# Delta-rule attention with a gated convolution: chunk 1's e from a cross gram, chunk 0's y from U where it lies, chunk 0's last level product on two PSUM banks, and a new order

## The chip, the cores and the metric

One core of a Trainium2 chip runs the whole kernel. Its engines are TensorE (PE, with its weight loads shown as PEld), VectorE (DVE), ScalarE (ACT) and GpSimd (POOL); SyncE (SP), ACT and POOL issue the DMAs. The metric is device time in microseconds (us), the median of several runs; lower is better.

## The reference, cut to what matters

For each of 4 batches and 8 heads (32 independent states of 48x48), 768 steps of a delta rule run in order. Its output, laid out as 768x384 for each batch, goes through a causal convolution of 5 taps, a sigmoid gate, and two 384x384 products:

```python
for t in range(S):
    y[:, :, t] = einsum('bhd,bhde->bhe', q[:, :, t], state)
    v_old = einsum('bhde,bhd->bhe', state, kt)        # kt: k over its norm
    state = state + bt * einsum('bhd,bhe->bhde', kt, vt - v_old)
...
gate = 1 / (1 + exp(-conv(x)))                        # x: y of all heads side by side
out = (gate * (x @ w_val)) @ w_out
```

All is float32.

## The kernel before, in words

**Chunks.** The 768 steps are cut into 12 chunks of 64, and two chunks make a group (6 groups). Inside a chunk the recurrence is solved with matrices: the gram of K with itself gives a triangular 64x64 system for each of the 32 states; its inverse XX times the right side gives U, and the state is a running sum of K^T U. A "pair" is two states that lie on the upper and lower 64 partitions, so most products are 16 pairs x 2 = 32 small matmuls; a float32 matmul shows as two records in the profile.

**Stages of group g.** `kp` (K with K, L399) and `qp` (K with Q, L427) for the first two groups, `kq` (both at once, L388) for the later ones. ACT and DVE bring the K gram into GL (`kpside` L405, `kpadd` L414), DVE masks the Q gram into AQ (`att0` L433, `att` L440), and SP copies AQ into R, the right operand of y (`stack_att` L920). Then `prep(g)` (L849), nearly all on DVE: transpose in (L493), 9 to 15 steps on 128x32 for norms and coefficients (L448), rows and merges of 16x16 inverses (L516 to L550), two transposes out (L552); POOL, ACT and SP scatter the results into G64, W64 and XAB.

**Stages of chunk ch.** `tri` (L892): products `m16`, `m32`, `lev1`, `lev2`, each followed by copies out of PSUM, fill XX[ch % 3]; the copies of `lev2` are `tevac` (L615). `chain` (L925): `e` = K times the state before the chunk (none for chunk 0), `eadd` on DVE adds it to V in VT, `u` = XX times VT, six copies `uevac` bring U into Y and US, `s` adds K^T U to the state that lies in two PSUM banks SPS, two copies `sevac` bring the state into the Y of the next chunk, `y` multiplies Q and the masked Q gram (R) with state and U, `yevac` and small DMAs bring y into X. Half of U lies in US on the partitions opposite to those where Y wants it; two DMAs (`stack("U")`, L692, "LU") carry it over before `y`. `moe` (L961) is the convolution (ACT `conv`, 4 DVE `tap`s), sigmoid, `val` and `outp` products and the store; chunks 0, 1, 10 and 11 run it for 64 columns, the others for two chunks together.

**The weights** arrive as float64 bits and are turned into float32 by DVE steps (L312 to L325, "f64"), ACT and two POOL products each (L330).

**Order.** All this is recorded as about 1,555 operations with their dependences, and `ORDER` (L41), a list of numbers, is the order in which they are emitted; so it fixes the order on each engine. A -1 in it is a warm-up matmul (`keep_warm`, L1024) that computes nothing needed. `BANKS` (L110) names which of the 6 free PSUM banks PB each product takes; a bank is taken again only when its readers are done. Each engine runs its list in order, so a waiting instruction holds what stands behind it. XX has three buffers: chunk 0 fills XX[0], chunk 1 XX[1], chunk 2 XX[2].

## Time and profile before

| | us |
|---|---|
| median of 3 runs | 290.45 (289.08 to 291.03) |
| the profiled execution, its own time | 289.44 |
| its span, first to last instruction | 287.7 |
| PE busy in the span | 255.3 (89%) |
| DVE busy | 215.5 (75%) |
| ACT busy | 175.4 (61%) |
| POOL busy | 133.9 (47%) |
| mean granted clock of TensorE | 0.958 of full speed (1.0 is 2.4 GHz, 0.5 is 1.2 GHz) |

Times in the rows count from the start of the profiled core. A row of the timeline is one instruction or a merged run of equal ones: start, busy time, engine, line, operation, output and inputs by tile name with sizes, count, and in brackets how long the engine had been idle and what released it. L229 is the ACT copy helper, L231 that of DVE and POOL, L250 all small matmuls, L1025 the warm-ups; so small operations are told apart by their tiles.

### The profile page before, as it was taken

The numbers are of one execution on the slowest core, as the hardware profiler recorded it, in microseconds if no ns is written. First come the engines' busy times: TensorE is split into PE (matmuls) and PEld (weight loads), VectorE is DVE, ScalarE is ACT, GpSimd is POOL, SyncE is SP. The second block draws the span as 40 slices with busy tenths as digits, with TensorE's granted clock in tenths as the row PEclk, the third lists the DMA queues.
The fourth block names the chain that finished last, engine by engine and source line by source line (L and its number), as shares of the span: only waits on it lengthen the run. The fifth ranks groups of instructions, "written<-read, shape, count | busy, mean of one in ns | idle before, by whom it ended". The sixth has DMA issues, their size and how long they took to land.

```text
span 287.7 us, 14508 instructions
## 1 busy us (share of the span) xinstructions
PE 255.3 (89%) x6272; PEld 194.2 (67%) x6272; DVE 215.5 (75%) x492; ACT 175.4 (61%) x403; POOL 133.9 (47%) x262
## 2 busy tenths in 40 slices
PE   7976485868989989899989869999999999999993
PEld 4975484768876868756768636777666776666861
DVE  6589998997979993769976974895998805831960
ACT  1677445847886645886535756756865728874531
POOL 8858692579257357057558830654053264000000
PEclk9979559899999999999999997999999999999999
DMA  6579872745664462477643771572234246302213
GB/s 179 168 207 229 212 215 62 204 117 126 178 149 137 137 165 52 106 190 184 166 116 90 218 195 43 146 190 57 68 95 139 70 108 188 95 11 71 91 55 82
DMA packets 33536, 38.22 MB, mean 133 GB/s; under 512 B 15680, under 2 KB 24000, under 8 KB 33472
## 3 DMA queue, kind: packets, MB, share of 16 engines
q1 hardware_dynamic: 27232, 24.07, 32.5%
q0 software_dynamic: 5120, 12.59, 16.1%
q8 instruction: 49, 0.80, 1.2%
q10 hardware_dynamic: 1120, 0.64, 0.8%
q14 instruction: 15, 0.12, 0.1%
HBM read 21.35 MB, written 4.72 MB: 91 GB/s over the span
## 4 chain that ended last, share of the span: by engine, by line
PE 43%; DVE 29%; issue 8%; ACT 6%; POOL 6%; DMA 5%; SPq 1%; DVEq 0%; ACTq 0%; POOLq 0%
PE PB L250 21%; PE PB L750 11%; PE PB L741 9%; DVE GT L732 4%; DVE TLP L493 3%; DVE AQ L431 2%; DMA Y<-US 2%; ACT XX L229 2%; PE SPT L250 2%; DMA KQ<-in_kf_dram 1%; DVE PR L544 1%; DMA GL<-GL 1%; POOL KQ L247 1%; DVE TT__82 L525 1%; DVE VT L676 1%
## 5 line engine op out<-in xcount | busy, mean ns | idle before, releaser
L732 DVE SCALAR_TENSOR_TENSOR GT<-X,CW,GT 128x256 f32<-128x256 f32 (+1 forms) x96 | 59.8, 645 | 21.0 <-ACT GT L229 17.0
L741 PE MATMUL PB<-X,WV 128*128 128x256 f32 (+1 forms) x144 | 52.5, 509 | 0.0
L750 PE MATMUL PB<-WO,GT 128*128 128x384 f32 x144 | 51.5, 498 | 0.0
L229 ACT ACTIVATE XX<-PB 32x512 f32<-32x512 f32 (+1 forms) x58 | 34.1, 589 | 15.7 <-PE PB L250 12.5
L741 PEld LDWEIGHTS PB<-X,WV 128*128 128x128 f32 x144 | 26.7, 194 | 15.7 <-issue 12.6
L750 PEld LDWEIGHTS PB<-WO,GT 128*128 128x128 f32 x144 | 26.0, 189 | 15.8 <-issue 0.7
L250 PE MATMUL PB<-KQ 48*64 48x64 f32 (+1 forms) x1024 | 28.4, 252 | 2.8 <-DVE AQ L431 1.2
L250 PEld LDWEIGHTS PB<-KQ 48*64 48x64 f32 x1024 | 24.3, 138 | 5.0 <-issue 2.2
L624 POOL TENSOR_TENSOR VT<-VT,NRM 128x384 f32<-128x384 f32 x24 | 20.5, 858 | 13.3 <-DMA VT<-in_vt_dram 12.6
L237 POOL DMA_DIRECT2D KQ<-in_kf_dram x32 | 16.7, 523 | 18.9 <-PE PB L250 18.7
L250 PE MATMUL PB<-KQ,Y 128*48 128x64 f32 (+2 forms) x768 | 24.7, 220 | 0.7 <-DMA Y<-US 0.7
L229 ACT ACTIVATE Y<-SPT 48x768 f32<-48x768 f32 (+1 forms) x22 | 17.7, 803 | 12.3 <-PE SPT L250 9.3
L250 PEld LDWEIGHTS PB<-KQ,Y 128*48 128x48 f32 (+2 forms) x768 | 22.6, 123 | 2.9 <-issue 1.6
L676 DVE TENSOR_TENSOR VT<-PB,VT 128x384 f32<-128x384 f32 x22 | 11.8, 552 | 16.1 <-PE PB L250 10.2
L231 POOL COPY G<-GL 16x512 f32<-16x512 f32 x24 | 17.0, 708 | 14.5 <-ACT GL L229 7.8
L250 PE MATMUL PB<-VT,XX 64*64 64x48 f32 x768 | 14.1, 221 | 9.0 <-ACT XX L229 3.7
L229 ACT ACTIVATE OS<-PB 128x384 f32<-128x384 f32 x24 | 11.6, 490 | 16.0 <-PE PB L750 13.0
L250 PEld LDWEIGHTS PB<-VT,XX 64*64 64x64 f32 x768 | 12.6, 135 | 12.9 <-issue 6.4
L229 ACT ACTIVATE GL<-PB 128x256 f32<-128x256 f32 x40 | 14.4, 384 | 11.3 <-PE PB L250 5.9
L250 PE MATMUL PB<-XAB,G 128*64 128x32 f32 x384 | 14.3, 235 | 7.2 <-DVE XAB L231 6.5
L431 DVE TENSOR_TENSOR AQ<-PB,MASK 128x256 f32<-128x256 f32 (+1 forms) x40 | 17.7, 467 | 3.6 <-PE PB L250 3.4
L250 PEld LDWEIGHTS PB<-XAB,G 128*64 128x64 f32 x384 | 13.5, 153 | 8.0 <-POOL W L231 6.6
(123 smaller groups left out, 509.1 us busy)
## 6 DMA issues: line engine op xcount, KB each, us to landing
KQ<-AQ SPq DMA_DIRECT2D x48, 128.0 KB, 4.3
KQ<-in_qr_dram POOLq DMA_DIRECT2D x32, 96.0 KB, 3.5
KQ<-in_kf_dram POOLq DMA_DIRECT2D x32, 96.0 KB, 3.1
VT<-in_vt_dram POOLq DMA_DIRECT2D x16, 192.0 KB, 3.6
KT<-in_kt_dram POOLq DMA_DIRECT2D x16, 192.0 KB, 3.8
out_dram<-OS SPq DMA_DIRECT2D x16, 192.0 KB, 2.1
Y<-US SPq DMA_DIRECT2D x23, 96.0 KB, 2.9
...
```

What stands on the lines that cost most here:

```text
L229: A.activation(out=out, in_=in_, func=AF.Copy, **kw)
L231: eng.tensor_copy(out=out, in_=in_)
L237: G.dma_start(out=dst, in_=src)
L247: eng.memset(t, x)
L250: PE.matmul(p, lhsT, rhs, start=start, stop=stop, tile_position=(row, col), skip_group_check=True)
L431: V.tensor_tensor(out=AQ[ch % NAQ][:, HB * h + u:HB * h + u + n], in0=p, in1=MASK[h].unsqueeze(1).to_broadcast([128, n, C]), op=ALU.mult)
L493: V.transpose(out=TL, in_=t.rearrange("p u x -> p x u"))
L624: G.tensor_tensor(out=v, in0=v, in1=n.unsqueeze(2).to_broadcast([128, HB, D]), op=ALU.mult)
L676: V.tensor_tensor(out=v, in0=bank["e", ch, h][:, 0:HB * D], in1=v, op=ALU.add)
L732: V.scalar_tensor_tensor(out=g, in0=XB[p % NX][:, m, :, lo + k:lo + k + n], scalar=CW[:, m, k:k + 1], in1=g, op0=ALU.mult, op1=ALU.add)
L741: PE.matmul(d[:, 0:B * n], WV[:, k, 128 * m:128 * m + 128], XB[p % NX][:, k, :, lo + 4:lo + 4 + n], start=k == 0, stop=k == NKT - 1)
L750: PE.matmul(bank["out", p, lo, i][:, 0:DM], g[:, i] if n == 2 * C else g[:, 2 * i:2 * i + 2].rearrange("p b t -> p (b t)"), WO[:, k, :], s ...
```

## The change

It has four parts. **Cross gram:** a new product `gx` early in the program multiplies K of chunk 1 with K of chunk 0 (32 small matmuls), and two ACT copies put it into GX, which is the buffer XX[2]. Chunk 1's `e` is now GX times U of chunk 0 (`ex`, 32 small matmuls), instead of K times the state after chunk 0; so it reads U's copies and no longer the state's. Since GX holds XX[2], the blanking of XX[2] (4 POOL fills) and with it the triangle of chunk 2 come after `ex`, and their entries in the plan stand behind chain(1). **First y:** chunk 0's `y` takes each half of U where `uevac` left it (Y or US), so the two LU DMAs of chunk 0 are gone; its two products are now split by position of the pairs (`crossed`), and their copies out are 6 instead of 3. **Two banks:** chunk 0's `lev2` writes its lower half into one bank and its upper half into another; ACT's two `tevac` read one, DVE's two the other. **Order:** `ORDER` and `BANKS` are new from their first to their last row (1604 entries for 1599, 45 warm-ups for 44).

```diff
 ORDER = [
-    38, 22, 39, 42, 35, 24, 40, 41, 7, 36, 37, 21, 48, 47, 16, -1, 49, 2, -1, 45, -1, -1, 235, -1, -1, 240, -1, -1,
...
-            yield bank["lev", ch, 2][r, C * j:C * j + C], TD[r, j, :], ZS[r, j, :], 64 * a, 64 * a
+            yield bank["lev", ch, 2 if ch or not a else 3][r, C * j:C * j + C], TD[r, j, :], ZS[r, j, :], 64 * a, 64 * a
...
-        p = bank["lev", ch, 2][q:q + 32]
+        p = bank["lev", ch, 2 if ch or not a else 3][q:q + 32]
...
+    GX = XX[NXX - 1]
+
+    def l_gx(i):
+        p = bank["gx", i]
+        for j in range(HB):
+            pp = HB * (j // QB) + QB * i + j % QB
+            for a in range(2):
+                f, w = spots(pp // HB, a), above(pp, a)
+                yield p[w:w + 64, C * j:C * j + C], KF[0][f:f + D, pp, :], KF[1][f:f + D, pp, :], f, w
...
+    def gxevac(i):
+        copy(A, GX.rearrange("p (h y j) x -> p h y (j x)", h=2, y=2)[:, :, i], bank["gx", i].rearrange("p (h y) -> p h y", h=2))
+
+    def l_ex(o):
+        p = bank["e", 1, o]
+        for j, pp in enumerate(crossed(o)):
+            for a in range(2):
+                w, h = above(pp, a), pp // HB
+                t = US[0][w:w + 64, h, D * (pp % QB):D * (pp % QB) + D] if pp % HB >= QB else Y[0][w:w + 64, w // 64, pp, :]
+                yield p[64 * a:64 * a + 64, D * j:D * j + D], GX[w:w + 64, pp, :], t, w, 64 * a
...
     def y(ch, h):
         p = bank["y", ch, h]
+        if ch == 0:
+            for j, pp in enumerate(crossed(h)):
+                for a in range(2):
+                    w = above(pp, a)
+                    t = US[0][w:w + 64, pp // HB, D * (pp % QB):D * (pp % QB) + D] if pp % HB >= QB else Y[0][w:w + 64, w // 64, pp, :]
+                    mm(p[64 * a:64 * a + D, C * j:C * j + C], t, R[0][w:w + 64, w // 64, pp, :], w, 64 * a)
+            return
...
+            if g == 0:
+                toks = [("gx", o) for o in range(2)]
+                add("PE", gx, (), r=k_of(0) + k_of(1), w=toks, take=toks)
+                for o in range(2):
+                    add("ACT", gxevac, (o,), r=[toks[o]], w=["GX"], give=[toks[o]])
...
-            add("PE", e, (ch,), r=k_of(ch) + [("Y", c2, "S", x, v) for x in range(2) for v in range(2)], w=toks, take=toks)
+            if ch == 1:
+                add("PE", ex, (), r=["GX"] + [("Y", 0, "U", 0, v, h) for v in range(2) for h in range(2)] + [("U", 0, h) for h in range(2)],
+                    w=toks, take=toks, kind="e")
+            else:
+                add("PE", e, (ch,), r=k_of(ch) + [("Y", c2, "S", x, v) for x in range(2) for v in range(2)], w=toks, take=toks)
...
-        for v in range(2):
+        for v in range(2 if ch else 0):
             add("ACT" if last and v else "SP", stack, ("U", ch, v), r=[("U", c2, h) for h in range(2)], w=[("Y", c2, "U", 1, v)], kind="LU")
...
+            for o, e_ in ((1, 1), (1, 0), (0, 0)) if ch == 0 else ():
+                add("ACT", yevac0, (h, o, e_), r=[t], w=[("YSB", 0)] if e_ else [("X", 0, 0, k) for k in ((1,) if o else (0, 2))], give=[t], kind="yevac")
...
-    for i in range(2, NXX):
-        blank_xx(i)
...
-        if ch + 2 < NCH:
+        if 1 < ch < NCH - 2:
             tri(ch + 2)
...
         chain(ch)
+        if ch == 1:
+            blank_xx(NXX - 1)
+            tri(2)
+            tri(3)
```

**Place 1: DVE at the start of prep(1).** GL_71 is the gram of group 1, AQ_67 and AQ_66 the masked Q grams of chunks 3 and 2, OS and X_91 raw weights. Before:

```order
L417 SCALAR_TENSOR_TENSOR GL_71<-PB_117,QUAD,GL_71 128x256
L431 TENSOR_TENSOR AQ_67<-PB_120,MASK_110 128x512
L431 TENSOR_TENSOR AQ_66<-PB_121,MASK_109 128x512
L493 STREAM_TRANSPOSE TLP<-GL_71 128x1024
L459 TENSOR_SCALAR SQ<-TLP 128x32
L453 RECIPROCAL REC<-SQ 128x32
```

After:

```order
L432 TENSOR_TENSOR AQ_67<-PB_117,MASK_109 128x512
L418 SCALAR_TENSOR_TENSOR GL_71<-PB_119,QUAD,GL_71 128x256
L326 TENSOR_SCALAR GT<-OS 128x384
L418 SCALAR_TENSOR_TENSOR GL_71<-PB_118,QUAD,GL_71 128x256
L418 SCALAR_TENSOR_TENSOR GL_71<-PB_120,QUAD,GL_71 128x256
L494 STREAM_TRANSPOSE TLP<-GL_71 128x1024
L432 TENSOR_TENSOR AQ_66<-PB_121,MASK_110 128x512
L460 TENSOR_SCALAR SQ<-TLP 128x32
```

Three of the four gram additions of group 1 stood inside prep(0) before and stand right ahead of prep(1)'s transpose now; a masking of chunk 2's Q gram (AQ_66) has moved between the transpose and the coefficient steps. On PE its product (`qp` of chunk 2) stood ahead of chunk 0's triangle and now stands inside it, between `m32` and `lev1`.

**Place 2: ACT at the end of chunk 0's triangle.** XX_74 and XX_75 are the buffers of chunks 0 and 1. Before:

```order
L229 ACTIVATE ZS<-PB_117 128x8x32
L229 ACTIVATE XX_75<-PB_120 128x2x8x32
L229 ACTIVATE TD<-PB_120,QUAD 128x8x32
L229 ACTIVATE XX_74<-PB_121 32x512 x2
L229 ACTIVATE TD<-PB_120,QUAD 128x8x32
```

After:

```order
L230 ACTIVATE XX_75<-PB_118 128x2x8x32
L230 ACTIVATE TD<-PB_118,QUAD 128x8x32
L230 ACTIVATE XX_74<-PB_121 32x512
L230 ACTIVATE TD<-PB_118,QUAD 128x8x32
L230 ACTIVATE XX_74<-PB_121 32x512
```

The order on ACT is nearly the same; DVE's two copies into XX_74 read PB_121 too before, and PB_117 now.

**Place 3: DVE around chunk 1's eadd** (VT_65 is chunk 1's V). Before:

```order
L532 TENSOR_TENSOR PR_83<-TLP,TT__82 128x256
L676 TENSOR_TENSOR VT_65<-PB_118,VT_65 128x384
L676 TENSOR_TENSOR VT_65<-PB_117,VT_65 128x384
L325 TENSOR_SCALAR GT<-OS 128x384
L537 TENSOR_REDUCE ZT<-PR_83 128x2x32
```

After:

```order
L523 TENSOR_TENSOR PR_83<-TT__82,TLP 128x144
L526 TENSOR_REDUCE TT__82<-PR_83 128x4x6
L321 TENSOR_SCALAR OS<-OS 128x384
L712 TENSOR_TENSOR VT_65<-PB_117,VT_65 128x2x192
L712 TENSOR_TENSOR VT_65<-PB_119,VT_65 128x384
L523 TENSOR_TENSOR PR_83<-TT__82,TLP 128x196
```

The two additions stood behind the last row of prep(1) and most of its first merge; they stand ahead of the last row now.

## Rows read from the trace of the kernel before

**Rows 1.** Windows: stretch and length; busy us (instructions) by engine; clock, DMA.

```profile
32.00:38.00 6.00, 5.30 (x95) 5.33 (x96) 5.80 (x14) 3.24 (x8) 4.47 (x8) 0.50 0.63 143
...
69.00:110.00 41.00, 38.22 (x957) 30.70 (x958) 36.10 (x93) 29.34 (x71) 21.86 (x39) 1.00 0.56 144
110.00:250.00 140.00, 133.70 (x3474) 96.06 (x3472) 102.33 (x228) 88.94 (x206) 64.02 (x112) 0.99 0.49 126
```

**Rows 2.** Waits of PE from 26 to 69 us: total, times, longest.

```profile
PE PB L250 <- DVE XAB L231: 6.5, 1, 6.5
PE PB L250 <- ACT XX L229: 3.3, 2, 2.6
```

**Rows 3.** Timeline, DVE: two of three gram additions inside prep(0), a weight step.

```profile
20.31 0.48 DVE L417 SCALAR_TENSOR_TENSOR GL<-PB,QUAD,GL 128x256 f32<-128x256 f32 x1
...
21.11 0.48 DVE L417 SCALAR_TENSOR_TENSOR GL<-PB,QUAD,GL 128x256 f32<-128x256 f32 x1 [0.32 <-ACT GL L229]
...
31.62 0.40 DVE L318 TENSOR_SCALAR OS<-OS 128x384 f32<-128x384 f32 x1
```

**Rows 4.** Timeline, PE: two qp products, then lev1, lev2 of chunk 0 and a warm-up.

```profile
24.00 2.22 PE L250 MATMUL PB<-KQ 48*64 48x64 f32 x128 [0.20 <-DMA KQ<-in_qr_dram]
...
39.00 1.07 PE L250 MATMUL PB<-XX,GL 32*32 32x32 f32 x64 [0.69 <-ACT XX L229]
...
42.23 1.27 PE L250 MATMUL PB<-ZS,TD 64*64 64x64 f32 x32
...
44.19 0.49 PE L1025 MATMUL SPT<-ZW 128*128 128x128 f32 x2
```

**Rows 5.** Timeline: the copies of lev2(0) on DVE and ACT, then u(0) on PE.

```profile
45.16 1.40 DVE L231 COPY XX<-PB 32x512 f32<-32x512 f32 x2
...
46.59 1.20 ACT L229 ACTIVATE XX<-PB 32x512 f32<-32x512 f32 x2 [2.52 <-DVE XX L231]
...
47.32 1.20 PE L250 MATMUL PB<-VT,XX 64*64 64x48 f32 x64 [2.65 <-ACT XX L229]
```

**Rows 6.** Timeline: chunk 1 from the last copies of U to its own u.

```profile
49.96 1.01 ACT L229 ACTIVATE Y<-PB 64x192 f32<-64x192 f32 x3
...
53.05 1.10 PE L250 MATMUL PB<-KQ 48*64 48x128 f32 x32
...
53.16 1.63 ACT L229 ACTIVATE Y<-SPT 48x768 f32<-48x768 f32 x2 [1.00 <-PE SPT L1025]
...
54.84 1.33 PE L250 MATMUL PB<-Y,KQ 48*64 48x48 f32 x60 [0.52 <-ACT Y L229]
...
58.15 1.02 DVE L676 TENSOR_TENSOR VT<-PB,VT 128x384 f32<-128x384 f32 x2
...
58.85 1.15 PE L250 MATMUL PB<-VT,XX 64*64 64x48 f32 x64 [1.73 <-DVE VT L676]
```

**Rows 7.** Timeline: ACT's DMA issues ahead of chunk 2's e, e(2), chunk 2's m16.

```profile
63.45 1.63 ACTq L240 DMA_DIRECT2D X<-YSB  x2
...
67.21 1.50 PE L250 MATMUL PB<-Y,KQ 48*64 48x48 f32 x64
...
69.17 1.12 PE L250 MATMUL PB<-XAB,G 128*64 128x32 f32 x32 [0.45 <-ACT GL L229]
```

**Rows 8.** Timeline: the longest PE wait behind 69 us, and val before and after.

```profile
165.69 2.84 PE L741 MATMUL PB<-X,WV 128*128 128x512 f32 x6
...
171.05 1.14 PE L250 MATMUL PB<-VT,XX 64*64 64x48 f32 x62 [2.28 <-DVE GT L745]
172.12 4.54 PE L741 MATMUL PB<-X,WV 128*128 128x512 f32 x6
```

**Rows 9.** Timeline, DVE and POOL: one coefficient form alone and beside POOL.

```profile
14.24 0.19 DVE L459 TENSOR_SCALAR SQ<-TLP 128x32 f32<-128x32 f32 x1
...
39.80 0.82 POOL L624 TENSOR_TENSOR VT<-VT,NRM 128x384 f32<-128x384 f32 x1
...
39.84 1.43 DVE L459 TENSOR_SCALAR SQ<-TLP 128x32 f32<-128x32 f32 x1
```

More of the change, by code (lines that the diff above doesn't have):

```diff
@@ L696, in stack @@
             (aside if ch == NCH - 1 and v else load)(Y[ch % 2][to, v].rearrange("p (h y j) d -> p h y (j d)", h=2, y=2)[:, :, 1], US[ch % 2][other])
-        if what != "U":
+        elif ch == 0:
+            pick = lambda t: t[:, QB:3 * QB] if what else t.rearrange("p (s j) x -> p s j x", s=4)[:, 0:4:3]
+            load(pick(R[0][to, v]), pick(AQ[0][other if what else to]))
+        else:
             u = slice(HB * what, HB * what + HB)
@@ L703, in xcols, with yevac0 @@
         return XB[ch // 2 % NX][:, :, :, lo:lo + C]
+    def yevac0(o, h, e):
+        bs = slice(2, 4) if h != o else slice(0, 2)
+        y = bank["y", 0, o][0:112, 4 * C * h:4 * C * h + 4 * C].rearrange("p (b e x) -> p b e x", e=2, x=C)
+        x = xcols(0)[0:112]
+        if h == 0:
+            copy(A, x[:, 0:3:2, bs].rearrange("p k b t -> p b k t"), y)
+        elif e == 0:
+            copy(A, x[:, 1, bs], y[:, :, 0])
+        else:
+            copy(A, YSB[0][:, bs], y[:, :, 1])
     def yevac(ch, h, e):
@@ L777, in blank_xx @@
                 r = 64 * a + 32 * h
-                add("POOL", fill, (G, (XX[i][r:r + 32, HB * h:HB * h + HB, 32 - 32 * h:64 - 32 * h], 0.0)), w=[("XXz", i)], kind="zXX")
+                add("POOL", fill, (G, (XX[i][r:r + 32, HB * h:HB * h + HB, 32 - 32 * h:64 - 32 * h], 0.0)), w=[("XXz", i)] + ["GX"] * (i == NXX - 1), kind="zXX")
     for i in range(NR):
@@ L907, in tri @@
         add("ACT", zevac, (ch,), r=[t1], w=["ZS"], give=[t1])
-        add("PE", lev2, (ch,), r=["ZS", "ZSc", ("TD", 0), ("TD", 1)], w=[t2], take=[t2])
+        add("PE", lev2, (ch,), r=["ZS", "ZSc", ("TD", 0), ("TD", 1)], w=[t2] if ch else [t2, ("lev", ch, 3)], take=[t2] if ch else [t2, ("lev", ch, 3)])
         for h in range(2):
             for a in range(2):
-                add("ACT" if ch or not a else "DVE", tevac, (ch, h, a), r=[t2], w=[("XX", x, h, a)], give=[t2])
+                t3 = ("lev", ch, 2 if ch or not a else 3)
+                add("ACT" if ch or not a else "DVE", tevac, (ch, h, a), r=[t3], w=[("XX", x, h, a)], give=[t3])
     def load_v(ch):
@@ L922, in stack_att @@
             for v in range(2):
-                add("SP", stack, (h, ch, v), r=[("AQ", ch % NAQ, h, i) for i in range(2)], w=[("R", ch % NR, "A", v, h)], kind="LA")
+                add("SP", stack, (h, ch, v), r=[("AQ", ch % NAQ, x, i) for i in range(2) for x in ([h] if ch else range(2))], w=[("R", ch % NR, "A", v, h)], kind="LA")
     def chain(ch):
@@ L928, in chain @@
             toks = [("e", ch, h) for h in range(2)]
-            add("PE", e, (ch,), r=k_of(ch) + [("Y", c2, "S", x, v) for x in range(2) for v in range(2)], w=toks, take=toks)
+            if ch == 1:
+                add("PE", ex, (), r=["GX"] + [("Y", 0, "U", 0, v, h) for v in range(2) for h in range(2)] + [("U", 0, h) for h in range(2)],
+                    w=toks, take=toks, kind="e")
+            else:
+                add("PE", e, (ch,), r=k_of(ch) + [("Y", c2, "S", x, v) for x in range(2) for v in range(2)], w=toks, take=toks)
             for h in range(2):
-                add("DVE", eadd, (ch, h), r=[toks[h]], w=[("VT", ch % NVT, h)], give=[toks[h]])
+                add("DVE", eadd, (ch, h), r=[toks[h]], w=[("VT", ch % NVT, x) for x in ([h] if ch > 1 else range(2))], give=[toks[h]])
         toks = [("u", ch, o) for o in range(2)]
@@ L947, in chain @@
             t = ("y", ch, h)
-            r = us + [("Y", c2, "U", 1, v) for v in range(2)]
+            r = us + ([("Y", c2, "U", 1, v) for v in range(2)] if ch else [("U", 0, x) for x in range(2)])
             r += [("R", ch % NR, "A", v, h) for v in range(2)]
```

18 lines of the change are left out of this document (13 added, 5 removed), and 148 rows, old and new, of the table ORDER.

## The prediction

> **What bounds the kernel now.** First the windows [rows 1]. From 69 us on PE is busy 38.22 of 41 us and then 133.70 of 140 us: almost nothing but work done earlier can move the end. From 32 to 38 us its clock is at 0.50, and up to 69 us it stands still again and again. The waits [rows 2] say for what: 6.5 us for the end of prep(0) on DVE, 3.3 us for ACT's copies into XX. So this is a kernel with a long start that runs as a chain through DVE, ACT and PE, and a long rest that is bound by PE. A change is worth what it takes off the chain up to about 69 us, plus the PE work that it gets done before then, less what it adds to the rest. DVE is a second bound of the start: before 69 us it has hardly a pause, so a product that comes earlier helps only if DVE's list reaches its reader earlier.
>
> **The change, step by step.** All sums are made against the profiled execution, 289.44 us with a span of 287.7; the other 1.74 us I leave as they are. It lies 1.01 us below the median of the runs, 290.45.
>
> *Prelude, to the first m16.* Three gram additions leave prep(0)'s list, at 0.40 us each behind one another, with a wait of 0.32 [rows 3]: 1.52 us. Two weight steps enter, about 0.40 each: 0.8. One ACT copy that ran ahead of the needed ones goes, 0.38. Sum -1.1 us. The gram `gx` itself (32 small matmuls like a qp, half of the 2.22 us that two take [rows 4]) falls into the 6.5 us in which PE waits [rows 2]; its two ACT copies likewise. Cost nothing; without that cover 1.1 us.
>
> *Chunk 0's triangle.* m32(0) gains only 0.6 of the 1.1, as two POOL copies into W64 stand behind a weight product there. Then `qp` of chunk 2 comes between m32(0) and lev1(0). No row shows it at this place: the nearest is 1.1 us at full clock [rows 4]; at the half clock of this stretch [rows 1] it is twice that, 2.2. I take 2.2, since the restart is as cold as before, and a warm-up of 0.4 at half clock. It covers the 0.69 us that lev1 waited [rows 4], and some 0.5 us of waits behind. lev2(0) ends at 43.50 now; -0.6 + 2.6 - 0.7 - 0.5 = +0.8.
>
> *Two banks.* The four copies of lev2(0) now run one after the other: DVE's two begin 1.66 us after lev2's end, since DVE is busy, and ACT's two wait 2.52 us for them [rows 5]; u(0) starts 3.8 us after lev2. Side by side, ACT is the longer: 1.20 for two, 0.45 for another copy between, some 0.15 to start, so 1.8. Saved 2.0 (between 1.2, if DVE comes as late, and 2.4). u(0) moves by +0.8 - 2.0 = -1.2: about 46.1 instead of 47.32.
>
> *Cross gram.* From u(0) to e(1) pass 7.5 us now: copies of U until 50.97, s(0), two copies of the state of 0.8 each, e at 54.84 [rows 6]. `ex` needs the copies of U alone: 3.65 us after u(0), so at about 49.8, or 5.0 earlier. That is not yet a gain, because eadd is on DVE. DVE's list reaches prep(1)'s transpose 2.2 us earlier, and then holds behind the masking of chunk 2's Q gram until that late `qp` is done, near 40 us. Behind it 34 instructions up to eadd; at the mean of 0.39 (36.10 us for 93, [rows 1]) 13.2 us. So eadd at 53.2 instead of 58.15, two microseconds after its product is ready, and u(1) at 53.9 instead of 58.85.
>
> *To e(2) and m16(2).* Now ACT is late: behind u(1) stand 16 copies and 3 DMA issues (0.82 each [rows 7]) ahead of the two copies of the state; 16 x 0.4 + 2.5 + 1.6 = 10.5 from 55.1 brings e(2) to 65.6 instead of 67.21: -1.6. In the waits before it PE does both `kq` of chunk 5, which were behind it: 2 x 1.10 [rows 6], 2.2 us of the rest. m16(2) needs prep(1): 26 DVE instructions behind eadd, 11.4 us with two transposes, then 2 us of POOL copies and the usual slips, 67.8 instead of 69.17, so PE waits once more. The rest begins 1.4 us earlier with 2.2 us less in it: **-3.6 us**. Between the extremes -1 (DVE as late as now) and -6 (no wait for qp or m16(2)).
>
> *First y.* 32 matmuls as before; two LU DMAs fewer ahead of it, three ACT copies more, each on half the data. Hidden behind s and kq; if ACT is the late one, 3 x 0.4 us, which the count of 16 contains.
>
> *The rest, behind 69 us.* The same work in another order. One hole goes by the new order: u(6) waits 2.28 us for a gate on DVE, then the clock falls and a val takes 4.54 instead of 2.84 us [rows 8]. The transpose of prep(4) now stands behind u(6) and not ahead of that gate: up to -4.0. Against it, 17 warm-ups stand behind e(2) instead of 4, and a warm-up marks a place at which PE has nothing: 13 x 0.25 (0.49 for two records [rows 4]) = +2.9 to 3.3 at least. I take -1.0; bounds -4 and +3.3.
>
> Sum: 289.44 - 3.6 - 1.0 = 284.8; with the 1.01 to the median **285.9 us**.
>
> **The rivals.**
> (a) *DVE takes it back.* eadd and prep(1) end when they do now, and chunk 1's early e waits. For it: DVE's list is full from 20 to 68 us, and it gets a new wait for qp(2). Against: three maskings and the kq copies done there are work that is then missing later. Only the 2.2 us of kq remain, less the new holes: 290.45 - 2.2 + 1 = 289.2.
> (b) *Slower: DVE and POOL collide inside prep(1).* A step of 0.19 us took 1.43 us while a POOL product of 0.82 ran [rows 9]; there are two more such steps close by in that stretch. DVE's chain is what u(1) and m16(2) wait for, so if the new places of the eight POOL weight products hit its dependent steps four more times, at 1.2 us each, m16(2) is 4.8 us later than I have it: 72.6, 3.4 behind today, less 2.2 of kq, and 2.9 us of holes behind: 290.45 + 4.1 = 294.5. It decides from about three further hits. Against: the number of POOL products is the same, and the present order has its share of hits. By the Trainium skill, "SBUF — State Buffer", section "Who interferes with whom", a DVE instruction with two SBUF inputs and a GpSimd one that reads SBUF exclude each other, and the second waits for the whole first one; by that rule each hit costs up to a full POOL product, and the row agrees in size (1.24 us lost, 0.82 us product).
> (c) *It does more.* The clock recovers before qp(2), DVE does not hold, and the hole at u(6) goes without a new one: 289.44 - 6 - 3 + 1.0 = 281.5.
> (d) *e(1) does not come earlier*, because `ex` is held by GX: excluded but for the ACT copies of `gx`, which end some 25 us before.
>
> **How the numbers follow.** Forecast 0.47, around 285.9, its own range 283.5 to 287.8. (c) 0.10, (a) 0.26, (b) 0.15, (d) 0.02, near 290. A measurement of this kernel can tell about 1% from no change, 2.9 us. Faster by more: most of the forecast and (c), 0.55. Within 1%: (a), (d) and the slow edge of the forecast, 0.28. Slower: (b) and a tail of (a), 0.17. The range reaches from (c) to short of (b): 281.5 to 292.0.
>
> **What the profile after would show.** Right: chunk 1's e, reading XX, at 49 to 51 us; ACT's copies into XX at chunk 0 without a wait for DVE's; eadd some 2 us behind its product; u(1) at 53 to 55; DVE idle near 38 to 40 us for a PE product; e(2) near 65.6 and m16(2) near 67.8; fewer than 6 us of PE idle between 110 and 250 us. Wrong: m16(2) at 69 us or later, DVE steps of 128x32 above 1 us more often than now, or long PE idle behind 110 us, where the warm-ups stand.

## The result, and the profile after

The changed kernel takes **293.05 us** (median of 4, 292.9 to 294.15) against 289.76 (288.67 to 291.03) for the kernel before beside it: ratio 1.0145 [1.0100, 1.0191]. It is slower, by about 1.5%, where 285.9 was forecast. In a later run on another chip (a1_after) it took 293.15 (6 runs) against 290.67 (11 runs), ratio 1.0221 [1.0149, 1.0293]. A ratio leaves out runs that are over 1.5% above the fastest of their kernel, so it isn't always that of the medians, and the traces of t2_both and u2_state are of such runs. The profiled execution took 293.03 us, with a span of 291.3.

The windows after, same stretches and columns as [rows 1]:

```profile
32.00:38.00 6.00, 1.58 (x30) 1.61 (x32) 5.62 (x11) 4.63 (x12) 2.74 (x6) 0.50 0.58 143
69.00:110.00 41.00, 38.14 (x1019) 30.90 (x1020) 34.40 (x93) 28.36 (x69) 24.34 (x43) 1.00 0.58 151
110.00:250.00 140.00, 133.82 (x3434) 97.83 (x3433) 98.98 (x229) 91.06 (x205) 65.04 (x115) 1.00 0.48 126
```

From 69 us on PE is as busy as before; from 32 to 38 us it has 1.58 us of work instead of 5.30. So the loss lies ahead of 69 us. The waits of PE from 0 to 69 us, columns as in [rows 2]:

```profile
PE PB L251 <- DVE X L321: 5.0, 1, 5.0
PE PB L251 <- issue: 3.0, 2, 1.6
PE PB L251 <- DVE XX L232: 2.4, 1, 2.4
...
PE PB L251 <- ACT GL L230: 2.0, 1, 2.0
```

The wait for prep(0) is 5.0 instead of 6.5, but it ends later; the wait for XX is now for DVE's half; two waits are put down to nothing ("issue"), and one for ACT's copies of the first gram is new. PE's timeline at the points the forecast named:

```profile
36.42 3.85 PE L251 MATMUL PB<-XAB,G 128*64 128x32 f32 x64 [5.02 <-DVE X L321]
...
48.91 0.32 PE L251 MATMUL PB<-VT,XX 64*64 64x48 f32 x4 [0.59 <-ACT XX L230]
51.68 1.22 PE L251 MATMUL PB<-VT,XX 64*64 64x48 f32 x58 [2.45 <-DVE XX L232]
...
54.34 0.28 PE L251 MATMUL PB<-Y,XX 64*64 64x48 f32 x1
...
61.74 0.32 PE L251 MATMUL PB<-VT,XX 64*64 64x48 f32 x4 [1.45 <-issue]
...
69.48 0.49 PE L1092 MATMUL SPT<-ZW 128*128 128x128 f32 x2 [0.83 <-ACT Y L230]
69.90 2.00 PE L251 MATMUL PB<-KQ,Y 112*48 112x64 f32 x64
...
72.75 1.19 PE L251 MATMUL PB<-Y,KQ 48*64 48x48 f32 x64
73.98 1.12 PE L251 MATMUL PB<-XAB,G 128*64 128x32 f32 x32
```

These are m16(0) and m16(1); u(0) in two pieces; the start of chunk 1's e (it reads U in Y or US, and GX, which is an XX buffer); the end of u(1); a warm-up that waits for ACT's copies of the state, and y(1) behind it; e(2) and m16(2). m16(2) starts at 73.98, where [rows 7] has 69.17: 4.81 us later. Part of that is the start. The 18 records of the first nine warm-ups of PE, before and then after:

```profile
5.24 2.17 PE L1025 MATMUL SPT<-ZW 128*128 128x128 f32 x18
```

```profile
5.50 3.42 PE L1092 MATMUL SPT<-ZW 128*128 128x128 f32 x18
```

The same matmuls took 1.25 us longer, and the first gram product starts at 8.84 instead of 7.34, before anything that the change touches is waited for. In 17 traces of this study, counted alike, this start differs by 1.6 us from one execution to another (the table below), and all later work moves with it. So from here on times are counted from the first gram product. Then, in us:

| | forecast | measured |
|---|---|---|
| start of the first gram product | 0 | +1.5 |
| from there to m16(0) | -1.1 | +2.2 (25.36 to 27.58) |
| m16(0) to the end of u(0) | -0.1 | +0.75 |
| end of u(0) to m16(2) | -0.2 | +0.34 |
| m16(2) to the last product | -3.2 | -1.3 (212.00 to 210.71) |
| sum | -4.6 | +3.5 |

The spans differ by 3.6. The prelude is the largest miss. Two rows hide more than they show:

- Behind m16(0), the forecast had lev2(0) end 1.9 us later than before and u(0) end 2.0 us sooner behind it. Measured, lev2(0) ends 0.4 us sooner (10.79 before, 10.38 after), and u(0) ends 1.2 us later behind it (5.02, 6.20). That the row comes out near the forecast is luck. The late `qp` of chunk 2 is most of the first: it took 1.16 us at full clock (42.49), where 2.2 at half clock were counted.
- Behind u(0), e(1) starts 1.3 us after its end instead of 5.5, and u(1) 6.1 us after it instead of 10.3: the cross gram did what was forecast (6.6). From u(1) to m16(2) pass 14.9 us instead of 10.3, where 13.9 were forecast.

### The profile page after: what moved, and what is told of

The parts are those of the page before. It is cut to its first block, busy times and chain, and to the rows that moved or that the text cites. A ratio compares the mean times of both kernels' runs of the same rounds, so it can differ in the third digit from the quotient of the medians.

```text
span 291.3 us, 14623 instructions
## 1 busy us (share of the span) xinstructions
PE 260.4 (89%) x6338; PEld 200.3 (69%) x6338; DVE 210.2 (72%) x492; ACT 177.8 (61%) x408; POOL 134.3 (46%) x262
## 4 chain that ended last, share of the span: by engine, by line
PE 57%; DMA 5%; ACT 4%; POOL 4%; issue 3%; DVE 1%; SPq 1%; ACTq 1%; DVEq 0%; POOLq 0%
PE PB L251 25%; PE PB L794 15%; PE PB L803 14%; DMA Y<-US 3%; PE SPT L251 2%; PE SPT L1092 2%; DMA GL<-GL 1%; POOL G L232 1%; POOL W L232 1%; DVE GT L785 1%; ACT Y L230 1%; POOL XAB L232 1%; SPq L235 1%; DMA W<-WB 1%; ACTq L241 1%
## 5 line engine op out<-in xcount | busy, mean ns | idle before, releaser
L794 PE MATMUL PB<-X,WV 128*128 128x256 f32 (+1 forms) x144 | 51.3, 497 | 0.0
L230 ACT ACTIVATE XX<-PB 32x512 f32<-32x512 f32 (+1 forms) x60 | 35.4, 590 | 10.6 <-PE PB L251 6.7
L251 PE MATMUL PB<-KQ 48*64 48x64 f32 (+1 forms) x1088 | 33.5, 279 | 3.6 <-ACT GL L230 2.0
L251 PEld LDWEIGHTS PB<-KQ 48*64 48x64 f32 x1088 | 28.9, 163 | 8.1 <-issue 3.0
L251 PE MATMUL PB<-KQ,Y 112*48 112x64 f32 (+2 forms) x736 | 24.5, 222 | 1.1 <-DMA Y<-US 0.7
L251 PEld LDWEIGHTS PB<-KQ,Y 112*48 112x48 f32 (+2 forms) x736 | 22.1, 124 | 3.1 <-issue 1.5
L230 ACT ACTIVATE X<-PB 112x256 f32<-112x256 f32 (+2 forms) x26 | 11.9, 464 | 17.1 <-PE PB L251 16.4
L251 PE MATMUL PB<-VT,XX 64*64 64x48 f32 x768 | 15.1, 222 | 6.2 <-issue 3.0
L232 POOL COPY G<-GL 16x512 f32<-16x512 f32 x24 | 16.1, 672 | 7.1 <-ACT GL L230 6.2
L230 ACT ACTIVATE Y<-PB 64x192 f32<-64x192 f32 x48 | 14.8, 321 | 6.6 <-PE PB L251 5.3
```

What stands on the lines that cost most here:

```text
L230: A.activation(out=out, in_=in_, func=AF.Copy, **kw)
L232: eng.tensor_copy(out=out, in_=in_)
L251: PE.matmul(p, lhsT, rhs, start=start, stop=stop, tile_position=(row, col), skip_group_check=True)
L794: PE.matmul(d[:, 0:B * n], WV[:, k, 128 * m:128 * m + 128], XB[p % NX][:, k, :, lo + 4:lo + 4 + n], start=k == 0, stop=k == NKT - 1)
```

## The experiments

The trace of each kernel is that of one execution. From the second column on: start of the first gram product; then, counted from it, the start of m16(0), the end of prep(1)'s last transpose out on DVE, and the start of m16(2); the time from m16(2) to the last output product; the median with its number of runs; the ratio to the kernel before, run beside it on the same chip.

| kernel | first | m16(0) | prep(1) out | m16(2) | rest | median us (n) | ratio |
|---|---|---|---|---|---|---|---|
| before | 7.3 | 25.4 | 58.7 | 61.8 | 212.0 | 289.76 (4) | |
| after | 8.8 | 27.6 | 61.2 | 65.1 | 210.7 | 293.05 (4) | 1.0145 [1.0100, 1.0191] |
| a1_after | 8.5 | 27.6 | 61.3 | 65.3 | 210.5 | 293.15 (6) | 1.0221 [1.0149, 1.0293] |
| c1_table | 7.8 | 26.5 | 60.5 | 65.1 | 210.0 | 290.85 (10) | 1.0010 [0.9964, 1.0055] |
| c2_early | 8.2 | 24.1 | 58.1 | 64.7 | 208.6 | 290.73 (10) | 1.0020 [0.9977, 1.0063] |
| c3_xab | 7.5 | 22.7 | 57.9 | 63.9 | 209.4 | 291.44 (10) | 1.0070 [1.0022, 1.0118] |
| c4_hold | 7.8 | 22.6 | 59.2 | 62.2 | 211.5 | 290.3 (10) | 1.0030 [0.9984, 1.0076] |
| d1_nowarm | 8.4 | 23.1 | 60.1 | 63.0 | 212.1 | 291.76 (6) | 1.0142 [1.0103, 1.0182] |
| d2_state | 8.7 | 24.2 | 60.6 | 64.0 | 212.4 | 291.07 (6) | 1.0125 [1.0088, 1.0161] |
| d3_onebank | 7.5 | 22.7 | 58.9 | 62.1 | 212.7 | 290.51 (6) | 1.0102 [1.0053, 1.0150] |
| o1_oldorder | 7.5 | 25.6 | 58.4 | 61.5 | 213.6 | 291.25 (12) | 1.0069 [1.0027, 1.0111] |
| t1_tail | 8.2 | 27.6 | 61.8 | 66.3 | 211.8 | 292.09 (6) | 1.0188 [1.0098, 1.0279] |
| t2_both | 8.4 | 23.1 | 60.6 | 63.2 | 213.1 | 290.5 (6) | 1.0112 [1.0020, 1.0205] |
| g1_light | 7.5 | 22.7 | 59.6 | 62.4 | 219.7 | 298.36 (6) | 1.0403 [1.0351, 1.0454] |
| u1_prep | 7.3 | 22.8 | 56.7 | 62.4 | 211.0 | 288.85 (12) | 0.9981 [0.9935, 1.0027] |
| u2_state | 8.0 | 22.6 | 56.4 | 62.5 | 212.1 | 290.5 (12) | 0.9980 [0.9924, 1.0035] |
| u3_late | 7.6 | 27.6 | 59.4 | 64.2 | 209.6 | 293.11 (12) | 1.0075 [1.0030, 1.0119] |

The kernel before had medians from 289.0 to 290.67 on these chips, with single runs on one chip from 286.06 to 292.61. A microsecond is therefore read from the traces, and the times judge only the larger steps.

### Three causes in the prelude: c1_table, c2_early, c3_xab

Each of the three keeps the edit of the one ahead of it. **c1_table** gives ACT a one-element copy behind its first DMA issues:

```diff
-    ... 42, 41, 0, 236, ...
+    ... 42, -2, 41, 0, 236, ...
...
+            if n == -2:
+                A.activation(out=DUM, in_=ZW[:, 0:1], func=AF.Copy)
```

> The changed kernel with one more ScalarE instruction: a copy of one column, placed behind its four DMA issues, that waits for one semaphore only, so that the function table is loaded there and not behind the first gram product. Theory A (the start is one chain, and the time was lost in it ahead of chunk 0's first product): ACT's first copies of the grams start 1.28 us earlier, the transpose of prep(0) too, the first m16 begins at 35.1 instead of 36.4 us, and the time falls by 1.3 us, to 291.8. Rival R1 (the loss is in prep(1), where DVE waits for the late Q gram of chunk 2): the start gains the same 1.28 us but the time stays at 293. Rival R2 (the loss is the clock, which stays at half speed up to 7.8 us here and only to 4.7 before): the first m16 and the time follow the clock of the first 8 us in this run's trace and not the table.

ACT's timeline after, and then in c1_table:

```profile
10.10 1.28 ACT L230 ACT_TABLE_LOAD   x1 [10.10 <-PE PB L251]
11.40 1.57 ACT L230 ACTIVATE GL<-PB,QUAD 128x256 f32<-128x256 f32 x4
```

```profile
2.72 1.28 ACT L1104 ACT_TABLE_LOAD   x1 [2.72 <-issue]
4.02 0.20 ACT L1104 ACTIVATE DUM<-ZW 128x1 f32<-128x1 f32 x1
9.11 1.72 ACT L233 ACTIVATE GL<-PB,QUAD 128x256 f32<-128x256 f32 x4 [4.88 <-PE PB L254]
```

In the kernel before, the function table is loaded at 2.72 us, and the first copy follows at 8.55. In the new order ACT's first copy is one that reads QUAD as well, so it waits for two engines, and the load stands behind the first of these waits: 1.28 us of load fall onto the chain. In c1_table m16(0) comes 1.08 us earlier, and m16(2) does not (65.1). Of the 1.8 us between the two profiled executions (293.03 and 291.22), 1.0 is an earlier start; rival R2, the clock, holds for the start alone. By the Trainium skill, "ScalarE: Activation LUTs", section "What ACT_TABLE_LOAD costs", a load takes about 1283 ns; the row agrees.

**c2_early** moves DVE's masking step `mask1(0)` to the front of DVE's list, and POOL's two fills, of YS and XAB, ahead of the second mask:

```diff
-    ... 56, 43, 54, 23, ... 79, 17, 80, ... 240, 18, ... 91, 12, 3, ...
+    ... 56, 43, 17, 54, 23, ... 79, 80, ... 240, 12, 18, ... 91, 3, ...
```

> As c1_table, and DVE's step for the first mask stands ahead of the gram additions again, as in the kernel before, with POOL's two memsets of 128x1024 moved ahead of the second mask, so that they are over before DVE's short steps of prep(0). Theory A: the wait of 0.5 us for the second mask and the step of 128x15 that took 1.49 instead of 0.16 us both go; first m16 at 33.3 us, time 290.0. R1: m16 as in A, time 293. R2: no difference to c1_table beyond what the clock of the first 8 us makes.

POOL, then DVE, in the trace after:

```profile
10.72 0.16 POOL L270 MEMSET MASK<- 128x64 f32 x1
16.07 0.15 POOL L271 MEMSET MASK<- 128x64 f32 x1 [5.20 <-DVE MASK L283]
...
19.33 0.95 POOL L248 MEMSET YS<- 128x1024 f32 x1
20.22 0.95 POOL L248 MEMSET XAB<- 128x1024 f32 x1
```

```profile
15.73 0.28 DVE L283 SCALAR_TENSOR_TENSOR MASK<-MASK,IND,MASK 128x64 f32<-128x64 f32 x1
...
19.43 0.28 DVE L283 SCALAR_TENSOR_TENSOR MASK<-MASK,IND,MASK 128x64 f32<-128x64 f32 x1 [0.51 <-POOL MASK L281]
...
19.71 1.49 DVE L319 TENSOR_SCALAR X<-X 128x15 f32<-128x15 f32 x1
```

A step of 0.28 us stands behind prep(0)'s transpose in DVE's list, POOL idles 5.20 us for it, and everything POOL has to do arrives 5 us later: DVE waits for the second mask, and two fills now meet a short step of DVE's chain. In the kernel before they ran beside other DVE steps (from 24.40 us on), with no loss that shows. The step of 128x15 takes 0.17 us in c2_early (at 17.21), and 1.49 here. m16(0) came 2.40 us earlier.

**c3_xab** puts ACT's copy into XAB (the one that m16(0) reads) ahead of a weight step, ZS and two W copies, and DVE's ahead of a gram addition:

```diff
-    ... 262, 75, 121, 253, 76, 123, 120, 267, ... 183, 119, 184, ...
+    ... 262, 119, 75, 121, 76, 123, 120, 253, 267, ... 183, 184, ...
```

> As c2_early, and ACT's copy into XAB for chunk 0 stands directly behind the transposes, not behind a weight step, the copy into ZS and two copies into W; on DVE its XAB copy stands ahead of one gram addition. Theory A: first m16 another 1.2 us earlier, at 32.1, time 288.9, about that of the kernel before (289.8). R1: first m16 at 32.1 but the time at 292 to 293.

The late copy on ACT in the trace after; in the kernel before it started at 31.86:

```profile
35.71 0.61 ACT L230 ACTIVATE XAB<-XA 64x512 f32<-64x512 f32 x1
```

It ends at 36.32, and m16(0), which reads it, starts 0.1 us later; the DVE weight step to which the profile puts down the wait ended at about the same time. In c3_xab m16(0) started 1.44 us earlier. It starts at +22.66 now, 2.7 us earlier than in the kernel before: with all three repaired, the prelude gives more than the 1.1 us forecast. But of the 4.9 us gained at m16(0), 1.3 arrive at m16(2), and by the times the three kernels don't differ. The next limit takes over.

### The hold of DVE inside prep(1): c4_hold, u1_prep

DVE at the start of prep(1) after (the transpose and the masking of chunk 2's Q gram), and at its end:

```profile
39.91 1.94 DVE L494 STREAM_TRANSPOSE TLP<-GL 128x1024 f32<-128x1024 f32 x1
43.78 0.69 DVE L432 TENSOR_TENSOR AQ<-PB,MASK 128x512 f32<-128x512 f32 x1 [1.92 <-PE PB L251]
...
66.22 0.41 DVE L432 TENSOR_TENSOR AQ<-PB,MASK 128x256 f32<-128x256 f32 x1
...
67.15 0.40 DVE L432 TENSOR_TENSOR AQ<-PB,MASK 128x256 f32<-128x256 f32 x1
67.48 1.05 DVE L554 STREAM_TRANSPOSE XA<-TT__82 128x512 f32<-128x512 f32 x1
68.38 0.72 DVE L432 TENSOR_TENSOR AQ<-PB,MASK 128x256 f32<-128x256 f32 x2
69.03 1.04 DVE L554 STREAM_TRANSPOSE WB<-TT__82 128x512 f32<-128x512 f32 x1
```

DVE holds 1.92 us for the product of `qp`, and four maskings of later chunks, 0.36 to 0.41 each, stand ahead of the last transpose, whose result m16(2) needs. prep(1) takes 30.2 us from transpose to transpose, 28.2 before. **c4_hold** lets the two maskings of prep(1)'s start change places:

```diff
-    ... 493, 266, 190, 144, 329, 275, 233, 486, ... 336, 269, 337, ...
+    ... 493, 190, 233, 269, 144, 329, 275, 491, ... 336, 266, 337, ...
```

> As c3_xab, and the masking of chunk 2's Q gram, which stands directly behind prep(1)'s transpose and waits 1.9 us for a product, changes places with that of chunk 3, whose product is long done. Theory A: DVE has no wait there, prep(1) ends 2.6 us earlier, m16 of chunk 2 two us earlier, time 287.0. R1: the same step is the one that counts, so this is the first of the four to gain, 2.5 us against c3_xab. If neither, prep(1) is early but POOL or PE is late next, and the time is that of c3_xab.

prep(1) grew to 31.4 us: the square root on ACT, which prep needs, stands behind copies there (DVE waits 1.33 us for it), and a masking waited 1.24 us for PE. m16(2) came 1.6 us earlier all the same. In c3_xab y(1) and the kq behind it took 2.72 and 1.97 us, at a granted clock of 0.63; in c4_hold they took 2.00 and 1.10, at 1.00. So that gain is the clock, and not prep(1). **u1_prep** (with d1's edit below) puts the coefficient steps directly behind the transpose, the root first on ACT, and four maskings behind the last transposes:

```diff
-    ... 189, 270, 132, ... 233, 269, 144, 329, 275, 491, 33, 277, 146, ...
+    ... 189, 270, 275, 276, 277, 278, 132, ... 233, 144, 329, 33, 146, ...
...
-    ... 350, 351, 509, 405, 352, 312, ... 611, 314, 506, ...
+    ... 350, 351, 312, 314, 313, 509, 405, 352, ... 611, 506, ...
```

> c4_hold without the warm-up ahead of chunk 1's first y, and prep(1) in another order: its first coefficient steps directly behind its transpose (the square root first on ACT), the masking of chunk 3 behind them, and its last steps and transposes ahead of four maskings for chunks 4 and 5. Theory C (prep(1) on DVE sets m16 of chunk 2): its last transpose begins at 53.5 to 55 us behind the first gram product instead of 58.1, m16 of chunk 2 at 58 to 60 instead of 62.2, the time 2 to 3 us below c4_hold's 290.3: 287 to 288.5. Theory G (PE and ACT set it, through the copies of the state and the order y, kq, e): the transposes as early, m16 of chunk 2 not before 61, and the time within 1 us of c4_hold.

The end of prep(1) in u1_prep, on DVE:

```profile
61.32 0.69 DVE L554 TENSOR_REDUCE TT__82<-PR 128x64 f32<-128x512 f32 x1
62.04 1.05 DVE L557 STREAM_TRANSPOSE XA<-TT__82 128x512 f32<-128x512 f32 x1
62.95 1.00 DVE L557 STREAM_TRANSPOSE WB<-TT__82 128x512 f32<-128x512 f32 x1
63.81 1.39 DVE L435 TENSOR_TENSOR AQ<-PB,MASK 128x256 f32<-128x256 f32 x4
```

prep(1) takes 28.6 us, and its end is 2.1 us earlier than before: nearly what theory C has. m16(2) is still at +62.4, as theory G has it: PE's own list ahead of it (s(1), y(1), kq, e(2)) ends only then. y(1) and the ACT copy that it waits for:

```profile
64.68 2.00 PE L254 MATMUL PB<-KQ,Y 112*48 112x64 f32 x64 [1.81 <-ACT GL L233]
```

```profile
64.24 0.38 ACT L233 ACTIVATE GL<-PB 128x256 f32<-128x256 f32 x1 [1.76 <-DVE AQ L435]
```

y(1) does not read that gram, so by the plan it waits for the copy to free a bank; and the copy waits for the first of the four maskings that the edit put behind the transposes (63.81). By the ratio this and u2_state are the best versions: 288.85 (12 runs) beside 289.58 of the kernel before, ratio 0.9981 [0.9935, 1.0027]. The four parts of the change, repaired, give what the kernel before gave, and nothing beyond.

**u3_late** has u1's order in prep(1) (with the copies of the state as in u2_state) and the prelude as changed:

```diff
-    ... 134, 493, 266, 190, 144, 329, 275, 233, 486, 33, ...
+    ... 134, 493, 190, 144, 329, 233, 33, ... 279, 266, 486, 138, ...
```

> The changed kernel with its prelude as it is, without the warm-up ahead of chunk 1's first y, prep(1) reordered as in u1_prep and the copies of the state as in u2_state. If the prelude is half of the loss and prep(1) and PE's order the other half: m16 of chunk 2 at 62 us behind the first gram product instead of 65.1, and a time of 290 to 291 (the changed kernel 293.1, the one before 289.9). If the prelude is all of it: 293.

293.11 us, 4.3 more than u1_prep on the same chip. By the ratios, 1.0075 [1.0030, 1.0119] against 0.9981, the prelude is worth 0.9% of the 1.5 to 2.2% that the change lost, so about half; by the traces m16(2) stands at 65.1 in the changed kernel, at 64.2 here and at 62.4 in u1_prep. The profiled execution took 289.81, the second shortest of 12 (289.53 to 297.64), only 0.8 us above u1's; so its trace doesn't show what makes the median. That stays open.

### The parts in the old order: o1_oldorder

o1_oldorder is the change's plan (cross gram, first y, two banks) in the order of the kernel before. In it `gx` stands ahead of `qp` of chunk 2, `ex` behind lev2 of chunk 1, and eadd early in prep(1). Against the changed kernel its list begins:

```diff
 ORDER = [
-    36, 22, 37, 40, 35, 25, 38, 39, 7, 42, 41, 0, 236, ...
+    38, 22, 39, 42, 35, 24, 40, 41, 7, 36, 37, 21, 48, 47, 16, -1, 49, ...
```

> The changed code in the order of the kernel before: gx in place among the warm-ups ahead of chunk 2's qp, e of chunk 1 directly behind lev2 of chunk 1, its copies of U and of the inverse ahead of the state's, its addition ahead of a masking on DVE, lev2 of chunk 0 on two banks, the first y from U; everything else as before. Theory A (the redrawn order lost the time, ahead of the first m16 and behind u of chunk 1): first m16 at 32.4 as before, u of chunk 0 done a microsecond earlier, e of chunk 1 at 50, u of chunk 1 at 53 instead of 58.5, e of chunk 2 at 64, m16 of chunk 2 at 68 to 69, since prep(1) ends when it did, and a time of 287.5 to 289, at or below the kernel before. Rival R5 (the parts themselves cost, the extra gram, the six copies of the first y, the late blanks): first m16 later than 33 or the time above 291. Rival R6 (e of chunk 1 was the bound): m16 of chunk 2 at 65 and 286.

u(1) started at +49.0, before at +51.5; s(1) 1.6 us earlier; m16(2) only 0.3 earlier, as is the end of prep(1) (+58.4 and 58.7). m16(2) waits 0.84 us there, 0.45 before, which the profile puts down to ACT's copies of a gram in both. So in the old order the chain through e(1) isn't what m16(2) waits for, and the three parts gain almost nothing. The rest took 1.6 us more than before, 1.2 of it one pause of PE that is put down to nothing; with the ratio at 1.0069 the parts cost some tenths of a per cent even in the old order.

### Two banks: d3_onebank

d3_onebank is c3_xab with the last product of chunk 0's triangle on one bank again:

```diff
-    bank["lev", ch, 2 if ch or not a else 3]
+    bank["lev", ch, 2]
```

> c3_xab with both halves of chunk 0's last triangle product in one bank again, as in the kernel before, all else equal. By the forecast the two banks are worth 2.0 us at u of chunk 0. Theory A: DVE's copies are the late ones here (its first began 2.7 us behind the product), so that one bank only adds ACT's second copy: u of chunk 0, e and u of chunk 1 up to 1.2 us later, and nothing of it at m16 of chunk 2 and in the time, within 1 us of c3_xab. If the forecast's size holds, all of them 2 us later.

u(0) of c3_xab on PE, and of d3_onebank:

```profile
44.82 0.32 PE L254 MATMUL PB<-VT,XX 64*64 64x48 f32 x4 [0.58 <-DVE ROOT L484]
47.12 1.84 PE L254 MATMUL PB<-VT,XX 64*64 64x48 f32 x58 [1.98 <-DVE XX L235]
```

```profile
46.90 0.45 PE L254 MATMUL PB<-VT,XX 64*64 64x48 f32 x4 [2.67 <-ACT XX L233]
47.53 1.84 PE L254 MATMUL PB<-VT,XX 64*64 64x48 f32 x58 [0.19 <-DVE XX L235]
```

With two banks the first four records start 2.1 us earlier, and the other 58 wait 1.98 us for DVE's half. u(0) ends 0.45 us earlier (+41.54 against +41.98), where 2.0 was forecast. m16(2) isn't later with one bank (+62.1 against +63.9, nearly all of it c3_xab's slower clock), and the times don't differ. In the changed kernel itself DVE's copies start 3.15 us behind the end of lev2(0), which is the first line:

```profile
45.65 1.15 PE L251 MATMUL PB<-ZS,TD 64*64 64x64 f32 x32
...
49.95 0.69 DVE L232 COPY XX<-PB 32x512 f32<-32x512 f32 x1
...
50.93 0.70 DVE L232 COPY XX<-PB 32x512 f32<-32x512 f32 x1
```

lev2(0) ended at 46.80, and ACT's two copies were done at 48.81.

### PE's order behind u(1): d1_nowarm, d2_state, u2_state

**d1_nowarm** is c3_xab without the warm-up ahead of y(1), which waits for ACT's copies of the state; **d2_state** also takes those copies ahead of others on ACT; **u2_state** does the same on u1_prep.

```diff
-    ... 391, 406, -1, 353, 526, 408, ...
+    ... 391, 406, 353, 526, 408, ...
...
-    ... 304, 400, 195, ... 305, 398, 302, ... 505, 397, 308, ...
+    ... 304, 400, 398, 397, 401, 195, ... 305, 302, ... 505, 405, 308, ...
...
-    ... 405, 352, 208, 503, ... 316, 407, 723, 391, 406, 353, ...
+    ... 405, 352, 407, 406, 208, 503, ... 316, 723, 391, 353, ...
```

The first pair is d1, the second the core of d2 against d1, the third u2 against u1.

> c3_xab without the one warm-up product that stands on PE between the last kq and chunk 1's first y. It writes the bank of the state, so it waits for ACT's copies of the state, and everything behind it on PE waits with it: 1.9 us in c3_xab. Theory A2 (the time behind the prelude is lost between chunk 1's u and chunk 2's e, where PE stands behind that warm-up and ACT is late): both y and the last kq of chunk 5 run in that wait, chunk 2's e begins at 67.9 instead of 69.8, m16 of chunk 2 at 69.1 instead of 71.1, and the time is 2 us below c3_xab. Rival R3 (prep(1) on DVE and POOL sets m16 of chunk 2): e moves, m16 stays at 71. Rival R4 (the rest gives it back): m16 at 69.1 and the time as c3_xab.

> d1_nowarm, and ACT takes the copies of chunk 1's U ahead of those of the first y, and the two copies of the state ahead of three DMA issues and the kq copies; on PE chunk 1's s stands ahead of one kq. Theory A2: the copies of the state end 2 us earlier, e of chunk 2 at 66.5, m16 of chunk 2 at 68.2, where prep(1) is the next bound (its transposes end at 65.1, and 3.1 us passed from there to m16 in the kernel before); 0.9 us below d1_nowarm. R3: m16 not before 71. R4: the time as c3_xab.

> u1_prep, and ACT's two copies of the state stand ahead of one DMA issue and of three kq copies. Theory G: e and m16 of chunk 2 another microsecond earlier than in u1_prep, and the time with them. Theory C: no difference to u1_prep.

In d1 m16(2) moved from +63.9 to +63.0 and the rest from 209.4 to 212.1: nothing gained. In d2 it was at +64.0, in u2 at +62.5 beside u1's +62.4. In u2 the copies of the state were done at +54.7, in u1 at +58.8, and y(1) started at +57.1 and +57.4: in both it waits for ACT's copy of a gram (3.08 and 1.81 us). So without the warm-up, earlier copies of the state are not the limit. What d1 showed is a clock at half speed behind u(1), where the page of the kernel before has none at that place (window as in [rows 1]):

```profile
58.00:65.00 7.00, 6.03 (x100) 5.72 (x104) 5.93 (x15) 3.82 (x14) 3.04 (x3) 0.53 0.43 101
```

### The warm-ups of the rest: a1_after, t1_tail, t2_both

**a1_after** repeats the changed kernel; **t1_tail** is it without the 17 warm-ups behind m16(2); **t2_both** joins t1, d1 and c4. The diff shows the first of the 17.

```diff
-    ... 579, 676, 657, 681, 580, -1, 739, 533, ...
+    ... 579, 676, 657, 681, 580, 739, 533, ...
```

> The changed kernel itself, unchanged, timed again in more rounds. In its first trace the granted clock stayed at half until 7.8 us (4.7 in the kernel before), and its first gram product began at 8.5 instead of 7.0 us; in the eight experiments so far the first product began between 7.2 and 8.4 us. Theory B (1.5 us of the first difference was this start, which differs from execution to execution): against the kernel before the ratio comes out at 1.007 to 1.010, not 1.0145, and the first m16 stands 27.5 us behind the first gram product again, wherever that one begins. If the loss is all in the kernel: the ratio is 1.0145 again.

> The changed kernel without the 17 warm-up products behind m16 of chunk 2. By the forecast each marks a place at which PE has nothing to do. If so (theory D): within 0.5 us of a1_after, PE idle behind 69 us longer by about the 4 us that the warm-ups took. If they stand where PE has work (theory E): up to 4 us faster than a1_after. If they keep the clock up (theory F): stretches at half clock behind 110 us that a1_after does not have, and 1.7 us more for each.

> c4_hold (early table, early mask and memsets, ACT's copy into XAB first, the masking swapped) without the warm-up ahead of chunk 1's first y and without the 17 behind m16 of chunk 2. Theory A plus D: the first m16 22.7 us behind the first gram product, m16 of chunk 2 62 us behind it, the rest 211, time 289.5, as the kernel before. With theory E: 286 to 287, below both kernels.

Without the 17 warm-ups PE is idle instead and its clock falls, here in t1_tail:

```profile
143.00:146.40 3.40, 3.40 (x10) 1.44 (x12) 0.41 (x2) 1.80 (x7) 2.18 (x3) 0.55 0.28 60
```

The rest is 211.8 instead of 210.5, and the time 292.09 beside 293.15: no difference that can be told. The warm-ups mark the holes; they don't make them. a1_after began late again (8.5) and had m16(0) at +27.6 again, but its ratio is 1.0221, where theory B had 1.007 to 1.010: the start doesn't explain what the times lose. t2_both missed its forecast too: m16(2) at +63.2 instead of 62, a rest of 213.1 instead of 211, and 1.0112. The texts on record of c1_table and a1_after give the first product and the clock of the start about 0.3 us lower than the timelines do.

### Weight steps later: g1_light

g1_light is c4_hold with four weight steps and some of their followers moved behind prep(1), and without the warm-up of d1:

```diff
-    ... 334, 201, 191, 291, 517, 285, 202, 292, 203, 393, ...
+    ... 334, 191, 291, 517, 285, 292, 393, ...
...
-    ... 408, 313, 524, 608, ...
+    ... 408, 313, 201, 202, 203, 204, 524, 608, ...
```

> c4_hold without the warm-up ahead of chunk 1's first y, and with four of DVE's steps on a weight tile, and the two POOL products and the load that follow from them, moved from inside prep(1) to behind its last transpose. Theory C (prep(1) on DVE sets m16 of chunk 2, and not e and u of chunk 1): its last transpose 2.4 us earlier, at 55.8 us behind the first gram product instead of 58.1, m16 of chunk 2 at 60 instead of 62.2, and 1.5 to 2 us less in all. If ACT's copies of the state or e of chunk 2 set it: the transpose as early, m16 of chunk 2 unmoved.

The product that needs the weights, on PE:

```profile
76.86 1.65 PE L797 MATMUL PB<-X,WV 128*128 128x256 f32 x3 [5.90 <-DVE VT L718]
```

It waits 5.90 us, and the kernel takes 298.36. prep(1) didn't get shorter either (out at +59.6, where 55.8 was expected). The weight steps in prep(1) have a due time of their own; a light DVE list can't be had that way.

## Why the prediction was wrong, step by step

- **"Prelude, to the first m16": failed.** Forecast -1.1, measured +2.2 from the first gram product. The sum of what leaves and enters prep(0)'s list was made; what the new order does around it was not: the table load behind a wait (1.08 us by c1_table), the mask step that holds POOL (2.40, c2_early), the late XAB copy (1.44, c3_xab). Together 4.9 us, and without them the step would have been -2.7. The reading that m16(0) waits for DVE [rows 2] hid that ACT and POOL can be late for the same product.
- **"Two banks": mechanism right, size wrong.** 2.0 forecast, 0.45 measured by d3_onebank. The lower bound (1.2, "if DVE comes as late") was too high as well: [rows 5] give 0.76, from the end of DVE's copies (46.56) to u(0). DVE came later still, since its hold for `qp` and its coefficient steps stand ahead of the copies. The forecast contained that hold, but didn't carry it to the next thing that DVE owes.
- **"Cross gram": the mechanism came, its worth didn't.** e(1) starts 1.3 us behind the end of u(0) instead of 5.5 (forecast 2.5), and eadd at 57.91 instead of 58.15 [rows 6], in spite of a start and a prelude 3.7 us later. In o1_oldorder u(1) is 2.5 us earlier and m16(2) 0.3.
- **"To e(2) and m16(2)": the number nearly right, the binding chain not.** The forecast let ACT's copies of the state set e(2), and prep(1) set m16(2) with PE waiting once more. Measured, m16(2) starts right behind e(2), and the last piece of prep(1) that it reads, POOL's copy into XAB, was done 1.8 us earlier:

```profile
71.56 0.60 POOL L232 COPY XAB<-XA 64x512 f32<-64x512 f32 x1
```

  In all kernels in the new order but g1_light m16(2) starts within 0.15 us of the end of e(2), so PE's own list sets it. e(2) in turn is late because the warm-up that waits for the copies of the state stands ahead of y(1) and one kq: 3.1 us of work come behind that wait and not into it. In no term were the pause of 1.45 us inside u(1) and the clock, at half speed from 62.7 to 66.1 us: the two kq there took 3.00 us and not 2.2.
- **"The rest": -1.3 instead of -3.2.** The hole at u(6) [rows 8] went, as forecast:

```profile
171.81 1.15 PE L251 MATMUL PB<-VT,XX 64*64 64x48 f32 x64
172.89 2.84 PE L794 MATMUL PB<-X,WV 128*128 128x512 f32 x6
```

  No wait, and val at 2.84 instead of 4.54. The 13 more warm-ups were as many as counted. But PE from 69 to 250 us has pauses that the profile puts down to nothing, 4.4 us where the kernel before has 1.0:

```profile
PE PB L251 <- issue: 4.4, 6, 1.4
```

  The four of them above 0.6 us sum to 4.0 us, against 0.7 before. By an estimate from these numbers the rest would have been 4.6 us shorter without them in both kernels, and not 1.3. The forecast has no term for them; they are more than the miss of this step.

- **The rivals.** (a) came nearest in kind: eadd stands where it did on the clock (57.91 and 58.15), but its number started from an unchanged prelude. (b), more collisions of DVE and POOL in prep(1), is not what happened: the sign that the forecast names, DVE steps of 128x32 above 1 us in prep(1), comes twice in both traces (1.43 and 1.02 us before, 1.14 and 1.35 after). The slower side was right as a sign, for another reason, and the time lies above the range.
- **The start.** 1.5 us of the 4.8 at m16(2) are the start of this execution. The traces from the first product on explain 2.0 of the 3.3 us between the medians. Three of the four traces with the changed prelude start at 8.2 to 8.8, u3_late at 7.6, and the 12 others with any part of the change at 7.3 to 8.7: nothing shows that the change has a part in it.
